# Output product by one level of Strassen's scheme: seven half-size products for eight

## The chip, the core and the metric

The kernel runs on one core of one Trainium2 chip. A core has a matrix engine (TensorE, "PE" in the profile, with its weight loads shown as "PEld"), three engines for elementwise work (VectorE or "DVE", ScalarE or "ACT", GpSimd or "POOL"), a queue engine that issues DMAs (SyncE or "SP"), a scratch memory (SBUF, 128 partitions) and a small accumulation memory that the matrix engine writes (PSUM, eight banks of 128 x 512 float32). Every engine works through its own queue strictly in the order in which the program was written; engines wait for one another through semaphores.

The metric is the time of one execution on the device, in microseconds (us); lower is better.

## The reference

There are two stages. The first is a cross attention between `x` (8 batches, 8 heads, 512 tokens, 64 features) and `state` (8, 8, 32, 64), in both directions:

```python
a     = softmax(x @ state^T / 8)        # over the 32 states
xread = a @ state                       # 512 rows for each batch
a2    = softmax(state @ x^T / 8)        # over the 512 tokens
sread = a2 @ x                          # 32 rows for each batch
```

The rows of both, with the heads side by side, make 8 x (512 + 32) = 4352 rows of 512 features. The second stage is a gated feed-forward net over them:

```python
gate = np.maximum(x @ w_gate, 0.0)      # 512 -> 1536
val  = x @ w_val                        # 512 -> 1536
out  = (gate * val) @ w_out             # 1536 -> 512
```

Inputs and outputs are float32; the kernel multiplies in bfloat16 and accumulates in float32. The last line is the output product, which the change rewrites.

## The kernel before, in words

**Units.** The 1536 hidden features are cut into 12 blocks of 128 (`jf`). For one batch and one `jf`, `gv` makes gate and value for all 512 tokens (two times two matmuls with 512 columns, into two PSUM banks), `relu` moves the gate to SBUF on ACT, and `mult` multiplies it with the value on DVE and writes the block `h_sb[:, jf]`. This is a unit, and there are 12 for each batch. A ninth round of 12 units (`gvs`, 256 columns) does the 256 state rows of all batches together.

**Output product.** It runs 18 units behind (`lag`), in pieces between the units. For a batch it is a product of 512 tokens by 1536 features with a matrix of 1536 by 512. A piece is four matmuls of 512 columns (`out_mms`, L338), and 12 pieces make the batch: four groups of 128 tokens (`tsub`), each accumulated over 12 `jf` in one of two PSUM banks of the pool `ps_o`, then copied on ACT (`fin_x`, L346) and stored from SP. The gate and value banks come from another pool of six.

**Order.** Nothing reorders the work at run time. The opening (batches 0 and 1, and the first four units of batch 2) is a list of words, `program`, where `ga` and `gb` are halves of `gv`, `o.0.4` is piece 4 of batch 0, `c` and `u` with `co` and `uo` make and copy the matrix `U`, the states already multiplied by the gate and value weights, `xn.3` is `x_next(3)`, and so on. From unit 28 on (batch 2, `jf` 4) a loop runs unit by unit, and `at(b, jf, ...)` hangs other work behind a unit: `att_half` (scores of the next batch, `sc_ps`, L184, which need `xT` of that batch), `u_block`, `sr` (sums for the state rows, `sr_ps`, L238, which for batches 0 to 2 reads `xs`), `x_sort` (GpSimd copies `xb` of batches 0 to 2 into the single buffer `xs`, L226), `x_dma` (SP loads `xf`), and `x_next`, which converts `xf` to bfloat16 on GpSimd (L149) and then transposes it by a DMA issued from SP (L156), giving `xT`.

**End.** After the last unit come the state rows' product (24 matmuls of 512 columns), the last pieces of batch 7, and `out_last`, two chains of 12 matmuls with 256 columns (L364), so that the last store is a half-width one.

Of the kernel before, what the change touches and what calls it, by code (L numbers as in the profile page):

```python
# [16 lines left out]
def kernel(  # L17
# [282 lines left out]
    def gv(b, jf, kcs=(0, 1)):  # L300
        if jf == 0 and kcs[0] == 0:
            hsb[b] = hpool.tile([128, NF, S], BF16, name="h_sb", tag="h_sb")
        if kcs[0] == 0:
            held["gv", b, jf] = [bank("gv_ps"), bank("gv_ps")], hsb[b][:, jf], S
        for w in range(2):
            for kc in kcs:
                gv_mm(held["gv", b, jf][0], b, jf, w, kc)

    def gvs(jf):
        f0 = jf * 128  # L310
        ps = [bank("gv_ps"), bank("gv_ps")]
# [5 lines left out]
        held["gv", B, jf] = ps, hs_sb[:, jf], nt  # L317

# [8 lines left out]

    o_n = [0]

    def o_bank():  # L330
        o_n[0] += 1
        return bank("o_ps", o_n[0] % 2)

    def out_mms(src, b, tsub, jfs):
        if jfs[0] == 0:
            held["o", b, tsub] = o_bank()
        for jf in jfs:
            nc.tensor.matmul(held["o", b, tsub], src[:, jf, tsub * 128:(tsub + 1) * 128], wo_sb[:, jf],  # L338
                             start=(jf == 0), stop=(jf == NF - 1))

    def out_rows(b, tsub):
        return out[b * SP: b * SP + S].rearrange("(p q) m -> q p m", q=NC)[tsub]

    def fin_x(b, tsub):
        o_sb = opool.tile([128, d_model], FP32, name="o_sb", tag="o_sb")
        nc.scalar.copy(out=o_sb, in_=held["o", b, tsub])  # L346
        nc.sync.dma_start(out=out_rows(b, tsub), in_=o_sb)

    def fin_s(t2):
        outr = out.rearrange("(b s) m -> b s m", s=SP)  # L350
        o_sb = opool.tile([128, d_model], FP32, name="o_sb", tag="o_sb")
        nc.scalar.copy(out=o_sb, in_=held["o", B, t2])
        for bq in range(4):
            eng = nc.sync if bq % 2 == 0 else nc.scalar
            eng.dma_start(out=outr[t2 * 4 + bq, S:SP], in_=o_sb[bq * Ns:(bq + 1) * Ns])

    def out_last(b, tsub):

        n = d_model // 2
        for half, (eng, q) in enumerate(((nc.scalar.copy, nc.scalar), (nc.vector.tensor_copy, nc.sync))):  # L360
            cols = slice(n * half, n * half + n)
            ps = o_bank()[:, 0:n]
            for jf in range(NF):
                nc.tensor.matmul(ps, hsb[b][:, jf, tsub * 128:(tsub + 1) * 128], wo_sb[:, jf, cols],  # L364
                                 start=(jf == 0), stop=(jf == NF - 1))
            o_sb = opool.tile([128, d_model], FP32, name="o_sb", tag="o_sb")
            eng(out=o_sb[:, 0:n], in_=ps)
            q.dma_start(out=out_rows(b, tsub)[:, cols], in_=o_sb[:, 0:n])

    def out_part(b, i):  # L370
        tsub, q = divmod(i, 3)
        out_mms(hsb[b], b, tsub, list(range(4 * q, 4 * q + 4)))

    def out_piece(b, i):
        out_part(b, i)
        if i % 3 == 2:
            fin_x(b, i // 3)

# [3 lines left out]
    nc.vector.memset(stT, 0.0)  # L382
    state_dma(nc.sync, 0, 2)
    x_dma_cast(0, 2)
# [11 lines left out]
    x_dma_cast(2)  # L396
    state_dma(nc.gpsimd, 2, B)
    wo_dma(0, 6)
# [7 lines left out]

    warm_ps = bank("warm_ps", 0)

    def spin(n):
        for i in range(n):  # L410
# [6 lines left out]
             "c": c_unit, "co": c_out, "u": u_unit, "uo": u_out, "ga": lambda b, jf: gv(b, jf, (0,)),  # L417
             "gb": lambda b, jf: gv(b, jf, (1,)), "re": relu, "mu": mult, "o": out_part,
             "of": lambda b, t, eng: fin_x(b, t), "xn": x_next}
    program = """  # L420
# [3 lines left out]
    gb.0.0 co.0.1.0.act co.1.1.1.dve ga.0.2 co.1.1.0.act gb.0.2 re.0.0 re.0.2 ga.0.3 gb.0.3 mu.0.0 ga.0.1 mu.0.2  # L424
    re.0.3 gb.0.1 re.0.1 xT.1.0 xT.1.1 xo.1.0.act mu.0.3 xT.1.2 xo.1.2.act xT.1.3 mu.0.1 xo.1.1.dve stc.2.8.pool
    xo.1.3.dve c.0.2 co.0.2.0.act sc.1.0 co.0.2.1.dve c.1.2 co.1.2.0.dve sc.1.1 ex.1.0 co.1.2.1.act ga.0.5 gb.0.5
# [22 lines left out]
    def at(b, jf, f, *args):  # L449
        units.setdefault(NF * b + jf, []).append(lambda: f(*args))  # L450
# [90 lines left out]
```

## Time and profile before

| | |
|---|---|
| time, median of 3 runs | 232.9 us (232.83 to 234.4) |
| profiled execution, span from first to last instruction | 232.8 us |
| PE busy | 224.0 us (96%) |
| DVE busy | 143.0 us (61%) |
| ACT busy | 118.8 us (51%) |
| POOL busy | 33.7 us (14%), 43 instructions |

The profiled execution has a span of 232.8 us, and the fastest of the three runs took 232.83 us, so nothing of note lies outside the span. The profile gives for each group of instructions its line, engine, operation, output and inputs by the program's names, shape, count, busy time and mean duration in ns. Matmuls overlap in the records: the duration of one (379 ns with 512 columns) is longer than the distance from one to the next, which is read from the starts of a row of them. In a timeline, the first column is the start and the second the length of a run of instructions of one kind, in us from the span's start.

### The profile page before, as it was taken

The numbers are of one execution on the slowest core, as the hardware profiler recorded it, in microseconds if no ns is written. First come the engines' busy times: TensorE is split into PE (matmuls) and PEld (weight loads), VectorE is DVE, ScalarE is ACT, GpSimd is POOL, SyncE is SP. The second block draws the span as 40 slices with busy tenths as digits, with TensorE's granted clock in tenths as the row PEclk, the third lists the DMA queues.
The fourth block names the chain that finished last, engine by engine and source line by source line (L and its number), as shares of the span: only waits on it lengthen the run. The fifth ranks groups of instructions, "written<-read, shape, count | busy, mean of one in ns | idle before, by whom it ended". The sixth has DMA issues, their size and how long they took to land.

```text
span 232.8 us, 4731 instructions
## 1 busy us (share of the span) xinstructions
PE 224.0 (96%) x1908; PEld 109.7 (47%) x1908; DVE 143.0 (61%) x246; ACT 118.8 (51%) x224; POOL 33.7 (14%) x43
## 2 busy tenths in 40 slices
PE   6699999999999999999999999999999999999994
PEld 2335445434455454345543544354445544666543
DVE  3667988974689766766676768576767463222100
ACT  2368876655655535573555355544654344332221
POOL 7936210600032312003000300000000000000000
PEclk9659999999999999999999999999999999999999
DMA  7999999033713481392139313611311111111232
GB/s 101 167 194 196 219 211 266 11 84 97 227 46 93 81 265 63 80 250 80 48 92 223 138 48 90 135 48 45 90 48 45 49 45 45 49 46 45 82 101 90
DMA packets 36951, 25.21 MB, mean 108 GB/s; under 512 B 17249, under 2 KB 32353, under 8 KB 36929
## 3 DMA queue, kind: packets, MB, share of 16 engines
q1 hardware_dynamic: 25168, 16.78, 25.4%
q0 software_dynamic: 11424, 7.73, 21.1%
q10 hardware_dynamic: 336, 0.39, 0.7%
q8 instruction: 15, 0.25, 0.4%
q14 instruction: 8, 0.06, 0.1%
HBM read 18.35 MB, written 8.91 MB: 117 GB/s over the span
## 4 chain that ended last, share of the span: by engine, by line
PE 86%; DVE 5%; DMA 4%; POOL 2%; issue 1%; ACT 1%; DVEq 0%; POOLq 0%
PE gv_ps L297 36%; PE o_ps L338 35%; PE gv_ps L315 5%; PE up L272 4%; DMA wv_sb<-in_moe_w_val_dram 3%; DVE h_sb L326 2%; PE sr_ps L238 1%; PE sr_ps L243 1%; PE sc_ps L184 1%; DVE a_sn L200 1%; PE upc L272 1%; DMA out_dram<-o_sb 1%; PE xT_ps L167 1%; POOL wg_sb L118 1%; DVE cs L194 1%
## 5 line engine op out<-in xcount | busy, mean ns | idle before, releaser
L297 PE MATMUL gv_ps<-ans,U 128*128 128x512 bf16 x384 | 97.6, 385 | 0.8 <-DVE U L292 0.5
L338 PE MATMUL o_ps<-wo_sb,h_sb 128*128 128x512 bf16 x372 | 94.7, 379 | 0.0
L322 ACT ACTIVATE g_sb<-gv_ps 128x512 bf16<-128x512 f32 (+1 forms) x108 | 62.3, 578 | 55.9 <-PE gv_ps L297 44.8
L326 DVE TENSOR_TENSOR h_sb<-gv_ps,g_sb 128x512 bf16<-128x512 f32 x96 | 64.8, 687 | 34.3 <-ACT g_sb L322 30.4
L297 PEld LDWEIGHTS <-U 128*128 128x128 bf16 x384 | 34.9, 99 | 44.8 <-issue 9.1
L338 PEld LDWEIGHTS <-h_sb 128*128 128x128 bf16 x372 | 36.1, 98 | 41.3 <-issue 0.9
L346 ACT COPY o_sb<-o_ps 128x512 f32<-128x512 f32 x31 | 18.1, 585 | 22.3 <-PE o_ps L338 22.3
L282 DVE CAST U<-up 128x512 bf16<-128x512 f32 x35 | 22.5, 684 | 6.1 <-PE up L272 6.1
L282 ACT CAST U<-up 128x512 bf16<-128x512 f32 x37 | 19.9, 594 | 9.2 <-PE up L272 9.1
L149 POOL CAST xb<-xf 128x1024 bf16<-128x1024 f32 x10 | 10.1, 1040 | 58.6 <-DMA xf<-in_x_dram 58.6
L194 DVE TENSOR_REDUCE cs<-e_sn 128x16 f32<-128x512 bf16 x16 | 10.9, 681 | 8.6 <-ACT e_sn L188 8.6
L326 DVE TENSOR_TENSOR hs_sb<-gv_ps,g_sb 128x256 bf16<-128x256 f32 x12 | 5.1, 424 | 15.4 <-PE gv_ps L315 10.5
L188 ACT ACTIVATE e_sn<-sc_ps 128x512 bf16<-128x512 f32 x16 | 9.6, 600 | 7.5 <-PE sc_ps L184 7.5
L200 DVE TENSOR_TENSOR a_sn<-e_sn,rc 128x512 bf16<-128x512 bf16 x16 | 12.5, 780 | 0.5
L272 PEld LDWEIGHTS <-stT 64*32 64x32 bf16 x480 | 4.9, 91 | 11.1 <-issue 10.5
L250 DVE RECIPROCAL rr<-sr_ps 128x128 f32<-128x128 f32 x8 | 7.6, 955 | 3.9 <-PE sr_ps L243 3.9
L226 POOL COPY xs<-xb 128x2048 bf16<-128x2048 bf16 x3 | 5.8, 1942 | 25.8 <-PE sr_ps L238 25.8
L292 ACT CAST U<-upc 128x512 bf16<-128x512 f32 x14 | 7.6, 588 | 3.7 <-PE upc L272 3.7
L184 PEld LDWEIGHTS <-xT 128*128 128x128 bf16 x128 | 6.0, 101 | 4.2 <-DVE xT L173 0.8
L184 PE MATMUL sc_ps<-stT,xT 128*128 128x64 bf16 x128 | 6.9, 199 | 0.5 <-DVE xT L173 0.5
L272 PE MATMUL up<-wg_sb,stT 64*32 64x512 bf16 x144 | 7.4, 386 | 0.0
L315 PE MATMUL gv_ps<-br,wg_sb 128*128 128x256 bf16 x48 | 7.2, 273 | 0.0
(56 smaller groups left out, 132.2 us busy)
## 6 DMA issues: line engine op xcount, KB each, us to landing
out_dram<-o_sb SPq DMA_DIRECT2D x31, 256.0 KB, 2.4
xf<-in_x_dram SPq DMA_DIRECT2D x4, 1024.0 KB, 6.4
wg_sb<-in_moe_w_gate_dram POOLq DMA_DIRECT2D x6, 256.0 KB, 11.4
wv_sb<-in_moe_w_val_dram POOLq DMA_DIRECT2D x6, 256.0 KB, 10.9
wo_sb<-in_moe_w_out_dram POOLq DMA_DIRECT2D x2, 768.0 KB, 15.1
xb<-in_x_dram POOLq DMA_DIRECT2D x2, 512.0 KB, 11.1
xf<-in_x_dram POOLq DMA_DIRECT2D x1, 1024.0 KB, 18.2
xb<-in_x_dram POOLq DMA_DIRECT2D x2, 256.0 KB, 4.6
```

Of the source, the lines that this page charges most:

```text
L149: copy[eng](out=xb[b][:, :, hs].rearrange("p c h d -> p h c d"), in_=xf[b][:, hs])
L184: nc.tensor.matmul(ps[:, c, jj], xT[b][:, c, 2 * kc + jj], stT[:, b, 2 * kc + jj], start=True, stop=True)
L194: nc.vector.reduce_sum(out=cs, in_=e_v, axis=AX.X)
L200: nc.vector.tensor_tensor(out=a_sn[b][:, kc].rearrange("p c (h n) -> p (c h) n", n=Ns), in0=e_v, in1=held["rc", b, kc].to_broadcast([128, ...
L272: nc.tensor.matmul(dst[kc][q:q + 32], stT[r:r + 64, b, j, 32 * sl:32 * sl + 32], wsb[r:r + 64, j, lo:lo + n], start=True, stop=True)
L282: copy[eng](out=U[b][:, w, kc, lo:lo + 512], in_=held["u", b, w, lo][kc])
L297: nc.tensor.matmul(ps[w], U[b][:, w, kc, f0:f0 + 128], ANS[b][:, kc].rearrange("p c t -> p (c t)"), start=(kc == 0), stop=(kc == NK - 1))
L315: nc.tensor.matmul(ps[w][:, 0:nt], wsb[:, j, f0:f0 + 128], br[:, j].rearrange("p b n -> p (b n)"), start=(j == 0), stop=(j == NJ - 1))
L322: nc.scalar.activation(out=g_sb[:, 0:n], in_=ps[0][:, 0:n], func=AF.Relu)
L326: nc.vector.tensor_tensor(out=dst, in0=ps[1][:, 0:n], in1=held["g", b, jf][:, 0:n], op=ALU.mult)
L338: nc.tensor.matmul(held["o", b, tsub], src[:, jf, tsub * 128:(tsub + 1) * 128], wo_sb[:, jf], start=(jf == 0), stop=(jf == NF - 1))
L346: nc.scalar.copy(out=o_sb, in_=held["o", b, tsub])
```

## The change

The output product of a batch is cut into two halves in each direction: 512 tokens into A1/A2 (256 each), 1536 features into two sixes of blocks, 512 outputs into two times 256. Eight products of a quarter size each would make it; Strassen's scheme in Winograd's form makes it with seven products and fifteen sums.

- **Weight sums** (`w_sum`), four in all, once: `t1`, `t2w` on DVE and `t4` and the block `b12` (in place) on GpSimd, each 128 x 1536.
- **Operand sums** (`h_sums`, `h_last`), four for each batch, on GpSimd: `s1`, `s2`, a third one written over the block `a21`, and a fourth over `a12`. Each is cut in three instructions of 128 x 512: twelve for each batch. `h_sums` is issued after `jf` 7, 9 and 11 of its own batch, `h_last` after the second half product of the next round's slot list (step `n` = 3).
- **Products.** A product is two halves of 128 token columns; a half (`o_half`) is six matmuls of 256 columns. A batch has 14 halves, `n` = 0 to 13, spread over twelve slots (`SLOTS`), still 18 units behind. They accumulate in two banks, `w` and `z`, which go on across products.
- **Output sums.** Four ACT copies of `w` for each batch (as many as before) and three DVE additions of `z` (`o_add`, 128 x 512, new). A store takes 2 x 256 columns for 128 partitions, 256 KB as before.
- **State rows.** The same scheme with 42 matmuls of 256 columns, operand sums on DVE, interleaved at the end with the last seven halves of batch 7; the last store is a full one (256 KB).
- **Room.** `xin` has one buffer and no longer two; `st_f` holds two batches, the other six are cast by their DMA, which takes `stc.2.8.pool` away; `hs_sb` goes into the `h_sb` pool. `x_next` and the next `x_dma` move from `jf` 9 and 10 to `jf` 2 and 3 for batches from 5 on.

```diff
-    xin = pool("xin", 2)
+    xin = pool("xin", 1)
+    spool = pool("spool", 2)
...
+    def w_sum(n, eng):
+        out_, in0, in1 = ((t1, b12, b11), (t2w, b22, t1), (t4, b21, t2w), (b12, b22, b12))[n]
+        {"dve": nc.vector, "pool": nc.gpsimd}[eng].tensor_tensor(out=out_, in0=in0, in1=in1, op=ALU.subtract)
+
+    PRODUCTS = ("p1", "p2", "p6", "p5", "p7", "p4", "p3")
...
+    def h_sums(b, k, eng="pool", n=2):
...
+        tt(out=s_block(b, 1, i), in0=a21, in1=a22, op=ALU.add)
+        tt(out=s_block(b, 2, i), in0=s_block(b, 1, i), in1=a11, op=ALU.subtract)
+        tt(out=a21, in0=a11, in1=a21, op=ALU.subtract)
+
+    def h_last(b, eng="pool", n=2):
+        for k in range(HF // n):
+            i = slice(n * k, n * k + n)
+            a12 = h_block(b, 1, 0, i)
+            {"dve": nc.vector, "pool": nc.gpsimd}[eng].tensor_tensor(out=a12, in0=a12, in1=s_block(b, 2, i),
+                                                                    op=ALU.subtract)
...
+    def o_half(b, n):
+        p, c = PRODUCTS[n // 2], n % 2
+        a, w = {"p1": (h_block(b, 0, 0), b11), "p2": (h_block(b, 1, 0), b21), "p3": (h_block(b, 1, 0), b22),
+                "p4": (h_block(b, 1, 1), t4), "p7": (h_block(b, 0, 1), b12),
+                "p5": (held.get(("s", b, 1)), t1), "p6": (held.get(("s", b, 2)), t2w)}[p]
+        ps = acc(b, "w" if p in ("p1", "p6", "p7", "p4") else "z")
+        for i in range(HF):
+            nc.tensor.matmul(ps[:, HM * c:HM * c + HM], a[:, i, 128 * c:128 * c + 128], w[:, i],
+                             start=(c == 0 and i == 0 and p in ("p1", "p2", "p5")), stop=(i == HF - 1),
+                             skip_group_check=True)
...
+    def o_end(b, n):
+        if n == 1:
+            o_copy(b, "r1")
+        elif n == 3:
+            o_add(b, "r1")
+            o_store(b, "r1", 0, 0)
+            h_last(b)
+        elif n == 5:
+            o_copy(b, "r2")
+        elif n == 9:
+            o_copy(b, "r3")
+            o_add(b, "r3")
+            o_store(b, "r3", 1, 1)
+        elif n == 11:
+            o_copy(b, "r4")
+            o_store(b, "r4", 1, 0)
+        elif n == 13:
+            o_add(b, "r2")
+            o_store(b, "r2", 0, 1)
+
+    SLOTS = ((0,), (1,), (2,), (3, 4), (5,), (6,), (7, 8), (9,), (), (10, 11), (12,), (13,))
...
-    re.1.7 mu.1.5 re.1.4 o.0.0 c.0.5 ...
+    re.1.7 mu.1.5 re.1.4 hs.0.0 hs.0.1 o.0.0 c.0.5 ...
-    mu.0.11 ... re.1.11 o.0.1
-    mu.1.10 o.0.2 ex.2.1 mu.1.11 c.1.4 u.2.0.0 u.2.1.0 co.1.4.1.act o.0.3 nx.2.0 co.1.4.0.dve ...
+    mu.0.11 ... re.1.11 o.0.1 hs.0.2
+    ws.0.dve mu.1.10 o.0.2 ex.2.1 mu.1.11 ws.1.dve c.1.4 u.2.0.0 u.2.1.0 co.1.4.1.act o.0.3 nx.2.0 co.1.4.0.dve ...
-    of.0.0.act xn.3 aT.2.1 o.0.4 mu.1.8 re.1.9 mu.1.9 ao.2.1.act ga.2.0 ...
+    xn.3 ws.2.pool ws.3.pool aT.2.1 o.0.4 mu.1.8 re.1.9 mu.1.9 ao.2.1.act hs.1.0 hs.1.2 hs.1.1 ga.2.0 ...
...
-            at(s, 9, x_next, b + 1)
+            at(s, 9 if b == 3 else 2, x_next, b + 1)
-            at(s, 10, x_dma, b + 2, (nc.sync,))
+            at(s, 10 if b == 3 else 3, x_dma, b + 2, (nc.sync,))
...
-        if g >= lag:
-            out_piece(*divmod(g - lag, NF))
+        if b < B and jf in (7, 9, 11):
+            h_sums(b, (jf - 7) // 2)
+        out_slot(g - lag)
...
+    h_sums(B, 0, "dve", HF)
+    rest = [n for s in SLOTS[(NF * (B + 1) - 1 - lag) % NF + 1:] for n in s]
+    for p in ("p1", 0, 0, "p2", 0, "p6", "p5", 0, 0, "p7", "p4", 0, "p3", 0):
+        s_step(p) if p else o_step(B - 1, rest.pop(0))
```

More of the change, by code (lines that the diff above doesn't have):

```diff
@@ L326, in mult @@
         nc.vector.tensor_tensor(out=dst, in0=ps[1][:, 0:n], in1=held["g", b, jf][:, 0:n], op=ALU.mult)
[L328 to L339, printed above, removed]
@@ L357, in out_last @@
[L357 to L368, printed above, removed]
@@ L370, in out_part @@
[L370 to L377, printed above, removed]
+    wo_v = wo_sb.rearrange("p (k i) m -> p k i m", k=2)
+    b11, b12, b21, b22 = (wo_v[:, k, :, HM * m:HM * m + HM] for k in range(2) for m in range(2))
+    def w_sum(n, eng):
+        out_, in0, in1 = ((t1, b12, b11), (t2w, b22, t1), (t4, b21, t2w), (b12, b22, b12))[n]
+        {"dve": nc.vector, "pool": nc.gpsimd}[eng].tensor_tensor(out=out_, in0=in0, in1=in1, op=ALU.subtract)
@@ new lines, in o_step, with out_slot, s_end @@
+    def o_step(b, n):
+        o_half(b, n)
+        o_end(b, n)
+    SLOTS = ((0,), (1,), (2,), (3, 4), (5,), (6,), (7, 8), (9,), (), (10, 11), (12,), (13,))
+    def out_slot(u):
+        b, s = divmod(u, NF)
+        for n in SLOTS[s]:
+            o_step(b, n)
+    def s_end(p):
+        outr = out.rearrange("(b s) m -> b s m", s=SP)
+        r, t, m = {"p1": ("r1", 0, None), "p2": ("r1", 0, 0), "p6": ("r2", 0, None), "p7": ("r3", 1, None),
+                   "c22": ("r3", 1, 1), "p4": ("r4", 1, 0), "p3": ("r2", 0, 1)}[p]
+        if p in ("p1", "p6", "p7", "p4"):
+            held["sr", r] = opool.tile([128, 512], FP32, name="o_sb", tag="o_sb")
+            nc.scalar.copy(out=held["sr", r][:, 0:HM], in_=held["acc", B, "w"][:, 0:HM])
+        else:
+            nc.vector.tensor_tensor(out=held["sr", r][:, 0:HM], in0=held["acc", B, "z"][:, 0:HM],
+                                    in1=held["sr", r][:, 0:HM], op=ALU.add)
+        if m is not None:
+            for bq in range(4):
+                eng = nc.sync if bq % 2 == 0 else nc.scalar
+                eng.dma_start(out=outr[t * 4 + bq, S:SP, HM * m:HM * m + HM],
+                              in_=held["sr", r][bq * Ns:(bq + 1) * Ns, 0:HM])
@@ L380, with s_step @@
+    def s_step(p):
+        o_half(B, 2 * PRODUCTS.index(p))
+        if p != "p5":
+            s_end(p)
+        if p == "p2":
+            h_last(B, "dve", HF)
+        if p == "p7":
+            s_end("c22")
     ctx.enter_context(tc.manual_schedule())
@@ L382 @@
     nc.vector.memset(stT, 0.0)
-    state_dma(nc.sync, 0, 2)
+    state_dma(nc.sync, st_f, 0, 2)
     x_dma_cast(0, 2)
@@ L396 @@
     x_dma_cast(2)
-    state_dma(nc.gpsimd, 2, B)
+    state_dma(nc.gpsimd, st_b, 2, B)
     wo_dma(0, 6)
```

87 lines of the change are left out of this document (52 added, 35 removed).

## The prediction

> **What bounds the kernel now.** The page comes first: the busy line of each engine and the chain that ended last.
>
> ```profile
> span 232.8 us, 4731 instructions
> PE 224.0 (96%) x1908; PEld 109.7 (47%) x1908; DVE 143.0 (61%) x246; ACT 118.8 (51%) x224; POOL 33.7 (14%) x43
> PE 86%; DVE 5%; DMA 4%; POOL 2%; issue 1%; ACT 1%; DVEq 0%; POOLq 0%
> ```
>
> PE is the bound, and it holds 86% of the chain. POOL looks idle. But a share over the span hides where POOL is needed, so the stages come next (columns: length, then busy us and instructions of PE, PEld, DVE, ACT and POOL, then granted clock, DMA share, GB/s).
>
> ```profile
> 4.00:8.00 4.00, 2.27 (x38) 1.42 (x36) 1.45 (x6) 0.58 (x1) 4.00 (x7) 0.92 1.34 177
> 8.00:12.00 4.00, 2.76 (x48) 1.59 (x53) 3.17 (x8) 1.82 (x4) 3.54 (x5) 0.50 1.27 167
> 12.00:16.00 4.00, 3.82 (x56) 1.39 (x41) 2.73 (x5) 2.75 (x6) 1.48 (x2) 0.50 1.43 194
> 16.00:20.00 4.00, 4.00 (x31) 1.80 (x31) 2.08 (x3) 2.25 (x5) 1.62 (x2) 0.80 1.46 196
> 36.00:48.00 12.00, 11.51 (x152) 5.47 (x151) 11.09 (x18) 8.08 (x15) 3.86 (x3) 1.00 0.40 116
> 84.00:96.00 12.00, 12.00 (x84) 5.42 (x82) 9.19 (x17) 6.73 (x13) 2.02 (x2) 1.00 0.43 136
> ```
>
> From 84 us on PE has no gap, so matmul time taken out there comes out of the span. The other rows are kept for a rival.
>
> **What the matmuls give.** The end of the timeline shows both sizes without other work between.
>
> ```profile
> 218.90 3.40 PE L338 MATMUL o_ps<-wo_sb,hs_sb 128*128 128x512 bf16 x15
> 224.08 2.75 PE L338 MATMUL o_ps<-wo_sb,h_sb 128*128 128x512 bf16 x12
> 226.67 2.78 PE L364 MATMUL o_ps<-wo_sb,h_sb 128*128 128x256 bf16 x24
> 229.55 0.42 DVE L367 COPY o_sb<-o_ps 128x256 f32<-128x256 f32 x1 [10.81 <-DMA out_dram<-o_sb]
> L364 PE MATMUL o_ps<-wo_sb,h_sb 128*128 128x256 bf16 x24 | 2.8, 273 | 0.0
> ```
>
> The state rows' 24 matmuls of 512 columns take from 218.90 to 224.08: 0.216 us each. The 24 of 256 columns have 2.78 us less one duration of 0.273 for 23 steps: 0.109 each, half of the other. A half-size product does cost half, though each matmul loads its own weights.
>
> Before: 8 batches x 48 + 24 = 408 of 512 columns, 88.0 us. After: 8 x 84 + 42 = 714 of 256, 77.8 us. **-10.2 us** if nothing stalls. A piece of 0.863 becomes a half of 0.654, with 14 for 12.
>
> **What GpSimd gets.** Twelve two-input sums of 128 x 512 for each batch, and two weight sums of 128 x 1536. The trace has no two-input instruction on POOL. The nearest rows:
>
> ```profile
> L149 POOL CAST xb<-xf 128x1024 bf16<-128x1024 f32 x10 | 10.1, 1040 | 58.6 <-DMA xf<-in_x_dram 58.6
> L127 POOL CAST st_b<-st_f 128x768 bf16<-128x768 f32 x1 | 0.8, 822 | 6.7 <-DMA st_f<-in_state_dram 6.7
> L226 POOL COPY xs<-xb 128x2048 bf16<-128x2048 bf16 x3 | 5.8, 1942 | 25.8 <-PE sr_ps L238 25.8
> ```
>
> Two casts give (1040 - 822)/256 = 0.85 ns an element on 0.17 us. One input of 512 is 0.60 us: the low end, if a second stream is free. The high end is the longest POOL row, 1.94 us. I take two passes, 2 x 0.60 = **1.2 us**, as a sum reads twice what a cast reads, and likewise 2 x 1.48 = 2.95 us for 1536. Call the first p.
>
> [...]
>
> In steady state it fits. A batch has 12 x 1.2 + 2 x 1.0 = 16.4 us of POOL, while the period was 24.1 and becomes 22.9. In the opening it doesn't, because POOL's queue there also holds the weight sums, two batches' operand sums, the three sorts and two conversions, in written order. The rows of before that matter:
>
> ```profile
> 41.80 0.69 DVE L326 TENSOR_TENSOR h_sb<-gv_ps,g_sb 128x512 bf16<-128x512 f32 x1 [0.17 <-ACT g_sb L322]
> 44.41 1.89 POOL L226 COPY xs<-xb 128x2048 bf16<-128x2048 bf16 x1
> 45.97 1.04 PE L338 MATMUL o_ps<-wo_sb,h_sb 128*128 128x512 bf16 x4
> 47.50 1.04 PE L297 MATMUL gv_ps<-ans,U 128*128 128x512 bf16 x4 [0.49 <-DVE U L292]
> 65.30 0.63 PE L238 MATMUL sr_ps<-e_sn,xs 128*128 128x64 bf16 x16
> 73.33 0.64 PE L238 MATMUL sr_ps<-e_sn,xs 128*128 128x64 bf16 x16
> 74.09 1.89 POOL L226 COPY xs<-xb 128x2048 bf16<-128x2048 bf16 x1 [5.98 <-PE sr_ps L238]
> 75.93 2.02 POOL L149 CAST xb<-xf 128x1024 bf16<-128x1024 f32 x2
> 86.89 0.40 PE L184 MATMUL sc_ps<-stT,xT 128*128 128x64 bf16 x8
> 100.03 0.95 SPq L100 DMA_DIRECT2D xf<-in_x_dram  x1
> 124.20 1.08 SPq L100 DMA_DIRECT2D xf<-in_x_dram  x1
> xT<-xb SPq DMA_TRANSPOSE x5, 4.4
> ```
>
> Before, the first sort ran at 44.41, long before its reader `sr_ps` at 65.30. Now it is queued behind batch 1's nine sums. Step by step:
>
> - `h_last(0)` needs half 3 on PE, 45.97 less three savings of 0.21 plus 0.65, and its end: 46.2, and the sums `hs.0.2`, from 42.5 on: 46.1. Start 46.5.
> - Three sums 3.6, `x_conv(3)` 2.0, `ws.2` and `ws.3` 5.9: **58.0**, when the new `b12` is there for half 8.
> - Nine sums of batch 1, 10.8, and the first sort, 1.9: **70.7**. `sr_ps` starts at 70.8 in place of 65.30. PE itself would be there at about 66: 65.30, plus 1.3 for the DVE work below, less 0.6 saved by 11 halves for 9 pieces.
> - The second `sr_ps` follows 8.03 later, as before (4 halves for 3 pieces, equal): 78.8. The single buffer `xs` frees 0.76 after that, as the rows at 73.33 and 74.09 show: 79.6. Third sort 1.9, six sums 7.2 (`hs.2.1`, `h_last(1)`), `x_conv(4)` 2.0: 90.7; the transposing DMA lands 4.4 later: **95.1**. Before, the scores of batch 4 ran at 86.89. PE would come at 78.8 + 13.56 - 0.6 = 91.8.
>
> So PE is 8.2 us late there. In general this point is 66.3 + 24 p: 24 sums' worth lie on the path, and POOL decides from p of about 0.9 on.
>
> After that POOL catches up and PE bounds again. From 86.89 on before had 145.9 us. It loses 8.2 of the 10.2 (74 pieces and the state rows, 69.0, become 93 halves, 60.8).
>
> **DVE.** Three output sums for each batch at the 0.69 of `h_sb` make 2.1 us. DVE was 9.19 of 12 in the last stage row, 77%, and goes to 86%; still beside PE. `ws.0`, `ws.1` are 1536 elements in bf16. Bounds from DVE's rows, scaled by three:
>
> ```profile
> L200 DVE TENSOR_TENSOR a_sn<-e_sn,rc 128x512 bf16<-128x512 bf16 x16 | 12.5, 780 | 0.5
> L220 DVE COPY ans<-aT_ps 128x512 bf16<-128x512 bf16 x4 | 1.7, 414 | 0.0
> 44.70 2.13 DVE L200 TENSOR_TENSOR a_sn<-e_sn,rc 128x512 bf16<-128x512 bf16 x1
> 48.95 0.69 DVE L200 TENSOR_TENSOR a_sn<-e_sn,rc 128x512 bf16<-128x512 bf16 x1
> ```
>
> At most 2.1 us, at least 1.0 with the start cost taken once; I take 1.0, all operands being bf16 as in L220. With the first output sum that is 2.7 us ahead of the copy on which `gv_ps` waited at 47.50, less the 1.44 by which `a_sn` at 44.70 was stretched, +1.3. While POOL is later anyway this costs nothing; without that cover 2.1 us, as the 0.84 already saved there goes too.
>
> The stretched row matters: `a_sn` reads two SBUF operands, runs 0.69 at 48.95, and took 2.13 while the sort ran. There are two for each batch, and three fall into 48 to 91 us (batch 2's second, batch 3's two), now against a POOL queue that is full. The wait can fall on either engine, 0 to 2.1 us on POOL's path; I take **+1.0**.
>
> **The end.** The last addition is 0.69 in place of 0.42. The last store is 256 KB and not 128 KB:
>
> ```profile
> out_dram<-o_sb SPq DMA_DIRECT2D x31, 256.0 KB, 2.4
> out_dram<-o_sb SPq DMA_DIRECT2D x1, 128.0 KB, 1.8
> xf<-in_x_dram SPq DMA_DIRECT2D x4, 1024.0 KB, 6.4
> L367 ACT COPY o_sb<-o_ps 128x256 f32<-128x256 f32 x1 | 0.4, 372 | 0.7 <-PE o_ps L364 0.7
> ```
>
> That is +0.3 and +0.6. State product p4 accumulates on the bank that ACT has just to copy after p7, which PE can't cover: 0.37 and the hand-over, 0.6. Together **+1.5**. Copies on ACT are as many as before; the converting state load, the moved tiles and the moved loads I cost at nothing, since PE's own work covers them, unless `xf` comes late (6.4 us of landing against some 20).
>
> **Sum.** 95.1 + 145.9 - 8.2 + 1.5 + 1.0 = **235.3 us**, made against the span of 232.8; the median of the runs, 232.9, is the same within 0.1.
>
> **Rivals.**
> - **A, forecast: POOL's queue delays PE in the opening**, PE bounds later. T = 206.5 + 24 p, even with before at p = 1.1; 232 to 239 for 1.05 to 1.35. Chance 0.48.
> - **B, POOL's sums are cheap** (p below about 0.9). PE never waits for them: 232.8 - 10.2 + 1.5 + 2.1 = 226.2, and 225 to 229 around it. The one-input rate speaks for it; against it, two operands. Chance 0.27.
> - **C, the pauses also cost clock.** In the stage rows PE was busy 2.27 of 4 us, and then the clock stood at 0.50 for 8 us, until some 5 us of dense work had passed. A waits about 4 us before `sr_ps` and 3.3 before `sc_ps`: each would be followed by about 5 us at half speed, 2.5 us lost, so 240 us. Against it: gaps of 0.49 in all from 36 to 48 us left the clock at 1.00. Chance 0.18. [...]
> - **D, DVE becomes the bound**: two `a_sn` for each batch stretched by 1.44 as at 44.70 take DVE from 86 to 98% of a period, and PE then waits for free banks; five batches at 2.9 make up to 14 us, 240. But POOL's sums run from `jf` 7 to the next batch's `jf` 1, `a_sn` from `jf` 3 to 6. Chance 0.05.
> - **E, half-size matmuls don't cost half**: L364 says they do. Chance 0.02; at 10% more it would be +8.
>
> **How the numbers follow.** The bounds of 1% are 230.6 and 235.2, between them being about what measurement can't tell from no change. Slower: A's upper half 0.25, C 0.18, D and E 0.07, 0.50. Within 1%: A's middle, 0.20. Faster: B 0.27 and A's low end 0.03, 0.30. The range runs from B's 226 to C's 241, and A alone is 232 to 239.
>
> **What would show it.** Right: POOL busy without a break from about 46 to 91 us, PE waiting for POOL `xs` at the first `sr_ps` and for the transposed `xT` of batch 4, POOL sums of 1.1 to 1.3 us, later batches 1.2 us shorter than 24.1. Wrong: POOL sums under 0.9 us, or PE at 100% from 50 us on; then it is B. A clock under 1.00 after the waits is C; PE waiting for DVE in later batches is D.

## The result and the profile after

The changed kernel takes **242.36 us** (median of 4 runs, 241.87 to 242.79), the kernel before 233.47 us beside it: a ratio of **1.0374, 95% interval 1.0332 to 1.0416**. It is slower by 3.7%, and above the top of the forecast range. One execution of 799.4 us, of the kernel in "The loads alone", is left out of every figure below.

The page of the changed kernel: span, busy line, and the chain that ended last by engine.

```profile
span 241.0 us, 5460 instructions
PE 216.8 (90%) x2174; PEld 140.7 (58%) x2202; DVE 163.0 (68%) x278; ACT 119.9 (50%) x226; POOL 149.9 (62%) x140
PE 64%; POOL 18%; DMA 9%; DVE 4%; issue 3%; ACT 1%; ACTq 0%; DVEq 0%; POOLq 0%
```

PE does less work than before (216.8 us busy, before 224.0), and the span is 8.2 us longer. PE's share of the chain fell from 86% to 64%; POOL has 18% and the DMA 9%. So TensorE now waits. Its list of waits (engine, line, what it waited for: total us, how often, longest):

```profile
PE sr_ps L240 <- POOL xs L228: 3.4, 1, 3.4
PE gv_ps L299 <- DVE U L294: 2.8, 1, 2.8
PE gv_ps L299 <- DMA ans<-a_sn: 2.4, 1, 2.4
PE sc_ps L186 <- DMA xT<-xb: 1.6, 1, 1.6
...
PE ws_ps L388 <- ACT o_sb L446: 1.2, 1, 1.2
```

Before, TensorE waited 0.49 us for `U` and for none of the others. Each happens once, four of the five in the opening or in the round of batch 4. The rows of the timeline that set the points of the path (start, length, then what was waited for):

```profile
71.52 1.04 PE L240 MATMUL sr_ps<-e_sn,xs 128*128 128x64 bf16 x16 [3.38 <-POOL xs L228]
...
96.46 0.41 PE L186 MATMUL sc_ps<-stT,xT 128*128 128x64 bf16 x8 [1.65 <-DMA xT<-xb]
...
114.42 1.04 PE L299 MATMUL gv_ps<-ans,U 128*128 128x512 bf16 x4 [2.41 <-DMA ans<-a_sn]
115.30 1.29 PE L388 MATMUL z_ps<-t,s 128*128 128x256 bf16 x6
...
123.72 0.40 PE L186 MATMUL sc_ps<-stT,xT 128*128 128x64 bf16 x8
...
146.67 0.40 PE L186 MATMUL sc_ps<-stT,xT 128*128 128x64 bf16 x8
...
169.62 0.40 PE L186 MATMUL sc_ps<-stT,xT 128*128 128x64 bf16 x8
```

Read the first scores of each batch, `sc_ps`, as mile posts. From 146.67 to 169.62 a round takes 22.95 us: that is the new period, 1.2 under the 24.1 of before, and it holds from 123.72 on. The first state read starts at 71.52 (before 65.30), the scores of batch 4 at 96.46 (before 86.89). But the round from 96.46 to 123.72 takes 27.26, 4.3 more than the others. In it stands the wait for `ans`, 2.41, and the half product behind it (six matmuls, at 115.30) takes 1.29 where one otherwise takes 0.82. The stages show why (columns as in the prediction):

```profile
108.00:116.00 8.00, 5.53 (x60) 2.97 (x46) 4.21 (x7) 4.34 (x8) 7.84 (x8) 0.97 0.87 214
116.00:120.00 4.00, 3.95 (x44) 3.07 (x44) 1.08 (x2) 0.20 (x1) 4.00 (x4) 0.64 0.01 4
```

The granted clock, last but two, was 0.64 after the wait, though PE was busy for 3.95 of these 4 us. So of the 4.3 us, 2.4 are the wait and most of the other 1.9 the clock. One of the runs below ("The weight sums on VectorE") has nearly the same wait at this point without the fall of the clock:

```profile
114.28 1.04 PE L299 MATMUL gv_ps<-ans,U 128*128 128x512 bf16 x4 [2.68 <-DMA ans<-a_sn]
115.16 0.82 PE L388 MATMUL z_ps<-t,s 128*128 128x256 bf16 x6
```

There the granted clock stays at 1.00, and from this `gv_ps` to the next scores it takes 7.67 us, where the changed kernel takes 9.30. So 1.6 of the 4.3 are clock.

What made `ans` late stands in SyncE's queue. First the changed kernel, with the conversion on GpSimd and the `a_sn` on VectorE that the two transposing DMAs wait for; then the kernel before at the same point of its round:

```profile
100.52 2.02 POOL L151 CAST xb<-xf 128x1024 bf16<-128x1024 f32 x2 [5.08 <-DMA xf<-in_x_dram]
101.94 1.14 DVE L202 TENSOR_TENSOR a_sn<-e_sn,rc 128x512 bf16<-128x512 bf16 x1
```

```profile
102.57 1.71 SPq L158 DMA_TRANSPOSE xT<-xb  x1
104.33 1.19 SPq L404 DMA_DIRECT2D out_dram<-o_sb  x1
105.61 0.43 SPq L102 DMA_DIRECT2D xf<-in_x_dram  x1
106.14 0.82 SPq L404 DMA_DIRECT2D out_dram<-o_sb  x1
107.05 3.73 SPq L210 DMA_TRANSPOSE ans<-a_sn  x1
```

```profile
93.66 1.24 SPq L208 DMA_TRANSPOSE ans<-a_sn  x1
97.47 0.34 SPq L347 DMA_DIRECT2D out_dram<-o_sb  x1
97.91 2.07 SPq L156 DMA_TRANSPOSE xT<-xb  x1
100.03 0.95 SPq L100 DMA_DIRECT2D xf<-in_x_dram  x1
```

Before, the load of x (1 MB) followed the transposing DMA of `ans` by 6.4 us. Now the transposing DMA of `xT`, the load and two stores stand ahead of it. `a_sn` was done at 103.08, but `xT` waited in the queue for the conversion, which ended at 102.54, and `ans` was issued only at 107.05: 4.0 us lost. Its issue then takes 3.73 in place of 1.24, and it lands 7.3 us after it started, where the median of the five such DMAs of this run is 3.3. In the next round the load stands ahead of `ans` as well, but 4.3 us ahead (125.87 and 130.17), and the issue takes 1.29.

### The profile page after: what moved, and what is told of

It reads as the page before. It is cut to its first block, busy times and chain, and to the rows that moved or that the text cites. A ratio compares the mean times of both kernels' runs of the same rounds, so it can differ in the third digit from the quotient of the medians.

```text
span 241.0 us, 5460 instructions
## 1 busy us (share of the span) xinstructions
PE 216.8 (90%) x2174; PEld 140.7 (58%) x2202; DVE 163.0 (68%) x278; ACT 119.9 (50%) x226; POOL 149.9 (62%) x140
## 4 chain that ended last, share of the span: by engine, by line
PE 64%; POOL 18%; DMA 9%; DVE 4%; issue 3%; ACT 1%; ACTq 0%; DVEq 0%; POOLq 0%
PE gv_ps L299 28%; PE w_ps L388 12%; PE z_ps L388 11%; PE gv_ps L317 4%; DMA ans<-a_sn 3%; DVE h_sb L330 3%; DMA wv_sb<-in_moe_w_val_dram 3%; POOL s L361 3%; POOL h_sb L369 3%; POOL s L360 2%; POOL h_sb L362 2%; PE up L274 2%; DMA xT<-xb 2%; POOL xb L151 2%; PE sr_ps L240 2%
## 5 line engine op out<-in xcount | busy, mean ns | idle before, releaser
L330 DVE TENSOR_TENSOR h_sb<-gv_ps,g_sb 128x512 bf16<-128x512 f32 (+1 forms) x108 | 69.6, 657 | 35.7 <-ACT g_sb L326 20.4
L360 POOL TENSOR_TENSOR s<-h_sb 128x512 bf16<-128x512 bf16 x24 | 27.7, 1153 | 50.2 <-DVE h_sb L330 50.2
L369 POOL TENSOR_TENSOR h_sb<-h_sb,s 128x512 bf16<-128x512 bf16 x24 | 28.2, 1199 | 8.2 <-PE z_ps L388 8.2
L397 ACT COPY o_sb<-w_ps 128x512 f32<-128x512 f32 x32 | 18.8, 587 | 23.0 <-PE w_ps L388 19.8
L361 POOL TENSOR_TENSOR s<-s,h_sb 128x512 bf16<-128x512 bf16 x24 | 28.3, 1178 | 1.9
L362 POOL TENSOR_TENSOR h_sb<-h_sb 128x512 bf16<-128x512 bf16 x24 | 28.1, 1172 | 0.0
L388 PE MATMUL w_ps<-wo_sb,h_sb 128*128 128x256 bf16 x192 | 26.9, 277 | 0.5 <-POOL wo_sb L338 0.5
L388 PE MATMUL z_ps<-wo_sb,h_sb 128*128 128x256 bf16 x192 | 26.2, 273 | 0.2
L388 PEld LDWEIGHTS <-s 128*128 128x128 bf16 x204 | 20.1, 99 | 6.5
L401 DVE TENSOR_TENSOR o_sb<-z_ps,o_sb 128x512 f32<-128x512 f32 x24 | 16.4, 683 | 3.9 <-ACT o_sb L397 3.3
```

The source lines that it names most:

```text
L330: nc.vector.tensor_tensor(out=dst, in0=ps[1][:, 0:n], in1=held["g", b, jf][:, 0:n], op=ALU.mult)
L360: tt(out=s_block(b, 1, i), in0=a21, in1=a22, op=ALU.add)
L361: tt(out=s_block(b, 2, i), in0=s_block(b, 1, i), in1=a11, op=ALU.subtract)
L362: tt(out=a21, in0=a11, in1=a21, op=ALU.subtract)
L369: {"dve": nc.vector, "pool": nc.gpsimd}[eng].tensor_tensor(out=a12, in0=a12, in1=s_block(b, 2, i), op=ALU.subtract)
L388: nc.tensor.matmul(ps[:, HM * c:HM * c + HM], a[:, i, 128 * c:128 * c + 128], w[:, i], start=(c == 0 and i == 0 and p in ("p1", "p2", "p5" ...
```

## The experiments

Each kernel is the changed one with the edit shown, unless another is named. "Before" is the kernel before on the same chip, beside which each was timed; the ratios are to it.

**The sort first.** In the written opening the first sort stands ahead of batch 1's sums, where it needs nothing new.

```diff
-    re.1.7 mu.1.5 re.1.4 hs.0.0 hs.0.1 o.0.0 ...
+    re.1.7 mu.1.5 re.1.4 hs.0.0 hs.0.1 xs.0 o.0.0 ...
-    for b in range(3):
+    for b in range(1, 3):
         at(2, 4 + 2 * b, x_sort, b)
```

> The first sort (x_sort of batch 0) is written before batch 1's nine sums, in a stretch where POOL waits for DVE anyway (35 to 41 us). Theory POOL queue (the order of GpSimd's queue makes PE wait at the first sr_ps, 71.5 us, and through the third sort and the conversion of batch 4 at sc_ps, 96.5 us): the wait of 3.4 us at the first sr_ps goes, it starts near 68; sc_ps of batch 4 near 93; time 3 to 4.5 us less, 238 to 239.5. Rival, PE and DVE set the pace there: the first sr_ps moves but nothing after it, time within 1 us of 242.4.

Measured: 238.65 us, ratio 1.0214 (1.0174 to 1.0253), 3.7 us less than the changed kernel, as expected. From the timeline and from the list of waits:

```profile
67.88 0.63 PE L240 MATMUL sr_ps<-e_sn,xs 128*128 128x64 bf16 x16
```

```profile
PE sc_ps L186 <- DMA xT<-xb: 2.5, 1, 2.5
PE gv_ps L299 <- DMA ans<-a_sn: 2.3, 1, 2.3
```

The first state read starts without a wait, 3.6 us earlier, and the scores of batch 4 come 3.7 us earlier, at 92.72. The delay that POOL's queue makes in the opening reaches the end in full. The wait for `ans` stays as it was, so it has another cause.

**The weight sums on VectorE.** This takes 6.2 us out of POOL's queue.

```diff
-    xn.3 ws.2.pool ws.3.pool aT.2.1 ...
+    xn.3 ws.2.dve ws.3.dve aT.2.1 ...
```

> The two weight sums ws.2 and ws.3 run on DVE and not on GpSimd. Theory POOL queue: POOL's path to the first sr_ps loses 6.2 us (3.09 and 3.10), DVE gets two times 0.97; the first sr_ps waits no more, sc_ps of batch 4 is near 93, time 238 to 239.5. Rival, DVE is what holds PE in the opening: 2 us of added DVE work make it 243 to 244.5.

Measured: 241.73 us (239.42 to 244.06), ratio 1.0316 (1.0243 to 1.0388). The expected gain is not there. POOL was no longer waited for, yet the first state read came at 72.06. The timeline of VectorE and the waits show what took its place:

```profile
50.62 1.53 DVE L202 TENSOR_TENSOR a_sn<-e_sn,rc 128x512 bf16<-128x512 bf16 x1
52.07 0.41 DVE L222 COPY ans<-aT_ps 128x512 bf16<-128x512 bf16 x1
52.41 1.45 DVE L338 TENSOR_TENSOR t<-wo_sb,t2w 128x1536 bf16<-128x1536 bf16 x1
53.78 1.90 DVE L338 TENSOR_TENSOR wo_sb<-wo_sb 128x1536 bf16<-128x1536 bf16 x1
55.61 1.27 DVE L330 TENSOR_TENSOR h_sb<-gv_ps,g_sb 128x512 bf16<-128x512 f32 x2
```

```profile
PE gv_ps L299 <- DVE h_sb L330: 2.8, 3, 2.2
```

The two sums hold the `h_sb` behind them by 3.3 us, and PE waits 2.2 for it. The same work blocks VectorE and TensorE directly instead of late through POOL.

**Filling the pause.** Twelve matmuls of 512 columns that nothing reads stand before the first state read, 2.6 us. They add work; the output stays what it was.

```diff
     def sr(b):
+        if b == 0:
+            dummy = bank("dummy_ps")
+            for i in range(12):
+                nc.tensor.matmul(dummy, id128, wo_sb[:, 0], start=True, stop=True)
         sr_mm(b)
```

> Twelve matmuls of 512 columns whose result nobody reads (2.6 us of PE) are put just ahead of the first sr_ps. The output is the same. Theory POOL queue: they fall into PE's wait of 3.4 us and the time doesn't rise, 242.4 within 0.7, and is up to 1.5 lower if the pause cost clock there (granted clock 0.68 from 72 to 76 us goes to 1.00). Rival, PE is on the path there: plus 2.6, 245.

Measured: 242.82 us (242.77 to 243.25), ratio 1.0399 (1.0361 to 1.0438). Work of 2.6 us costs 0.5, and the intervals of the two ratios overlap. The timeline (this execution ran 1.5 us later from the opening on: its scores of batch 3 start at 67.77, those of the changed kernel at 66.23):

```profile
69.52 2.75 PE L559 MATMUL dummy_ps<-wo_sb,id 128*128 128x512 bf16 x12
73.07 0.64 PE L240 MATMUL sr_ps<-e_sn,xs 128*128 128x64 bf16 x16 [0.80 <-POOL xs L228]
73.54 0.63 PE L245 MATMUL sr_ps<-e_sn,sel 128*128 128x64 bf16 x16
```

The wait shrank to 0.80, and the state read's 16 matmuls took 0.64, against 1.04 after the wait of 3.38. So that wait did cost clock too, which was 0.68 from 72 to 76 us in the changed kernel: from the first state read to the second it is 9.11 us in the changed kernel, 8.31 here, 8.03 before. That is 0.8 us of clock for a wait of 3.4. It shows that PE had the slack. It doesn't show that the clock alone was worth anything for the end, as POOL was still late for what follows.

**The moved loads back.** Conversion and load of x stand where the kernel before has them.

```diff
-            at(s, 9 if b == 3 else 2, x_next, b + 1)
+            at(s, 9, x_next, b + 1)
-            at(s, 10 if b == 3 else 3, x_dma, b + 2, (nc.sync,))
+            at(s, 10, x_dma, b + 2, (nc.sync,))
```

> x_next and x_dma go back to jf 9 and 10 for all batches, as in the kernel before; one xin buffer stays. Theory, SP's order: the 1 MB load xf now stands ahead of the transposing DMA of ans in batch 4's round, which was issued at 107.05 and took 3.7 us to issue and 7.3 to land, so that gv_ps waited 2.4 us at 114 us, and the clock fell after it; with the load later the wait goes, time 4 us less, 238.5. Rival, that loss comes from DVE or POOL being late: time unchanged, 242.4, or higher because the conversion now comes late for the transposing DMA.

Measured: 242.23 us (241.83 to 243.46), ratio 1.0383 (1.0328 to 1.0439): nothing gained. The wait for `ans` is gone, but another came, in each later batch. The list of waits:

```profile
PE sc_ps L186 <- DMA xT<-xb: 4.8, 4, 1.8
```

There are four of them here; in the changed kernel it was one. The scores of batches 4 to 7 start at 96.71, 120.80, 144.91 and 168.97, 24.1 us apart. That is exactly the period of before: the conversion, now behind POOL's sums, takes back per batch what the products save. So the conversion had to be moved; what cost was the place of the moved DMAs in SyncE's queue. Here `ans` is issued at 102.94, as soon as `a_sn` is done (102.88), and lands within 3.2.

**The load behind `ans`.** Only the load, not the conversion, is put later, behind the transposing DMA.

```diff
-            at(s, 10 if b == 3 else 3, x_dma, b + 2, (nc.sync,))
+            at(s, 10 if b == 3 else 6, x_dma, b + 2, (nc.sync,))
```

> One move in SP's queue: x_dma of the batch after the next goes from jf 3 to jf 6, so that the 1 MB load stands behind the transposing DMA of ans (jf 5) and not ahead of it. Theory, the load ahead of it made ans late: the wait of 2.4 us of gv_ps at 114 us goes, and the clock stays at 1.00 after it (1.9 us): 238 to 239.5. Rival, ans is late because xT of batch 5 and the stores ahead of it wait (xf late at 100.5 us): the wait stays, 242.4.

Measured: 239.32 us (239.07 to 240.23), ratio 1.0237 (1.0196 to 1.0278), 3.0 us less in time; the span is 237.3, 3.7 less. SyncE's queue now:

```profile
104.69 1.73 SPq L404 DMA_DIRECT2D out_dram<-o_sb  x2
106.51 2.58 SPq L210 DMA_TRANSPOSE ans<-a_sn  x1
109.18 0.53 SPq L102 DMA_DIRECT2D xf<-in_x_dram  x1
```

The wait for `ans` is gone, the clock stayed at 1.00 from 108 to 132 us, and the scores of batch 5 start at 119.97, where they had been at 123.72. The other waits are the changed kernel's. `ans` still stands 3.1 us in the queue behind `xT` and two stores (`a_sn` is done at 103.45), and the slowest of the five `ans` DMAs lands after 5.4. So the load was not all of the delay, but enough of it for the wait to go. This is the part that the prediction had left out.

**The loads alone.** The kernel *before* with only the two moved lines of the change.

```diff
-            at(s, 9, x_next, b + 1)
+            at(s, 9 if b == 3 else 2, x_next, b + 1)
-            at(s, 10, x_dma, b + 2, (nc.sync,))
+            at(s, 10 if b == 3 else 3, x_dma, b + 2, (nc.sync,))
```

> The kernel before, with nothing of the change but the moved loads: the conversion of the next x (x_next) at unit 2 and the load behind it (x_dma) at unit 3 of each slice but one, as the changed kernel has them. Theory 'the load ahead in SyncE's queue costs the wait for ans by itself': TensorE waits 2 to 3 us for ans in the round of batch 4, the clock dips there, and the time goes up by 2.5 to 4.5 us, to 236 to 238. Rival 'it takes GpSimd's sums too': without them GpSimd is free, xf(4) is converted earlier, the load behind it is issued and landed before the transposing DMA of ans is, and the time stays within 1 us of 233.5.

Measured: 234.20 us (median of nine runs), ratio 0.9993 (0.9968 to 1.0018): no difference. Its queue at the same place:

```profile
89.67 1.29 SPq L100 DMA_DIRECT2D xf<-in_x_dram  x1
91.22 0.42 SPq L347 DMA_DIRECT2D out_dram<-o_sb  x1
93.45 1.24 SPq L208 DMA_TRANSPOSE ans<-a_sn  x1
```

The load stands ahead of `ans` here too, but 3.8 us ahead and not 1.4, and the issue of `ans` takes its 1.24. So the rival was right: the order alone costs nothing. The rows suggest that it needs POOL's late conversion: the load and `ans` stand in the queue behind the `xT` of that conversion, which ended at 88.26 here, 1.5 us after the scores of batch 4 began (86.72), but at 102.54 in the changed kernel, 6.1 after them (96.46). This kernel also keeps two buffers for `xf`, which was not tried apart; but in both kernels the load is issued behind that `xT`, when a buffer is free with one as with two. Which of the load and the stores beside it slowed the transposing DMA was not tried apart either.

**The end.** One output slot stands between state products p7 and p4, so that ScalarE can copy p7 meanwhile.

```diff
-    for p in (..., "p5", 0, 0, "p7", "p4", 0, "p3", 0):
+    for p in (..., "p5", 0, 0, "p7", 0, "p4", "p3", 0):
```

> In the order of the end, half 12 of batch 7 goes between state products p7 and p4, so that ACT copies the bank of p7 meanwhile. Theory: the wait of 1.2 us at ws_ps goes or shrinks, time 0.5 to 1.2 less, 241.2 to 241.9. Rival, the last store and not PE sets the end, or the o_sb buffers do: unchanged within 0.3.

Measured: 243.02 us (241.26 to 244.27), ratio 1.0383 (1.0318 to 1.0447): no gain, though the four runs spread over 3.0 us, more than the gain looked for. The traces are clearer: the wait before p4 fell from 1.2 to 0.6, and from the scores of batch 7 to the end it is 71.4 us in both (169.62 to 241.0, 171.05 to 242.5). SyncE's queue of this kernel at the end:

```profile
236.14 3.08 SPq L453 DMA_DIRECT2D out_dram<-o_sb  x6
239.31 0.39 SPq L404 DMA_DIRECT2D out_dram<-o_sb  x1
```

The six small stores of the state rows hold the queue for 3.08 us, and the last large store follows right behind them. That these stores and not TensorE set the end is what the rows suggest; no run moved the stores.

**The repairs together.** The sort first, the load behind `ans`, the order at the end (as in the edits above), and for batch 4 the load (`xd.4`) and the conversion behind it earlier.

```diff
-    re.1.7 mu.1.5 re.1.4 hs.0.0 hs.0.1 o.0.0 ...
+    re.1.7 mu.1.5 re.1.4 hs.0.0 hs.0.1 xs.0 o.0.0 ...
-    xn.3 ws.2.pool ...
+    xn.3 xd.4 ws.2.pool ...
-    at(2, 4, x_dma, 4, (nc.sync,))
...
-            at(s, 9 if b == 3 else 2, x_next, b + 1)
+            at(s, 4 if b == 3 else 2, x_next, b + 1)
-            at(s, 10 if b == 3 else 3, x_dma, b + 2, (nc.sync,))
+            at(s, 6, x_dma, b + 2, (nc.sync,))
```

> First sort early as in e1, x_dma behind ans as in e5, the end as in e6, and x_dma of batch 4 right behind x_next(3), x_next(4) at jf 4 of batch 2 (ahead of the other sorts), x_dma of batch 5 at jf 6. Theory, POOL's and SP's order cost what the losses of PE say: sc_ps of batch 4 waits no more (2.5 us in e1), the ans wait and its clock go (4.3), the end shrinks by about 1: 238.7 less 6.5 to 8, 231 to 232.5, about even with before or a little faster. Rival, the cost is POOL's amount of work and not its order: the waits turn up at other places and it stays above 235.

Measured: 234.02 us (10 runs), ratio **1.0000** (0.9976 to 1.0024). Of the waits listed for the changed kernel only VectorE's 2.8 for `U` and 0.6 before p4 are left. The scores of batch 4 start at 92.34. The loss of the change, 8.3 us, is gone, so it came from the order in two queues; without it the change is worth nothing. The expectation, 231 to 232.5, was missed, and so was its rival, above 235. What the earlier load and conversion of batch 4 give by themselves was not timed.

**The weight sums earlier as well.** The edit is made to the kernel of the repairs. `ws.0` and `ws.3` stand behind `co.1.5.0`, `ws.1` behind the copies of the third slice's first unit.

```diff
-    ... co.1.5.0.dve gb.0.10
+    ... co.1.5.0.dve ws.0.dve ws.3.pool gb.0.10
-    ws.0.dve mu.1.10 ... mu.1.11 ws.1.dve c.1.4 ... co.1.4.0.dve uo.2.0.0.1.dve
+    mu.1.10 ... mu.1.11 c.1.4 ... co.1.4.0.dve uo.2.0.0.1.dve ws.1.dve
-    xn.3 xd.4 ws.2.pool ws.3.pool aT.2.1 ...
+    xn.3 xd.4 ws.2.pool aT.2.1 ...
```

> As e7, and the weight sums moved: ws.0 earlier on DVE, ws.3 on GpSimd ahead of hs.0.2, where POOL waits for DVE, ws.1 behind the copies of U on DVE. Theory: PE's wait of 2.8 us for U at 48.8 us shrinks by 1.5 to 2.5, 229 to 231, faster than before by 1 to 2%. Rival, DVE's amount of work in 36 to 52 us holds PE whatever the order: no gain over e7.

Measured: 233.13 us (10 runs), ratio **0.9958** (0.9933 to 0.9982). This is the best version, and its gain is 0.4%; 229 to 231 was expected. PE's wait for `U` did not shrink, it grew from 2.8 to 3.05. The rows of PE and VectorE around it:

```profile
49.51 1.89 PE L299 MATMUL gv_ps<-ans,U 128*128 128x512 bf16 x4 [3.05 <-DVE U L294]
```

```profile
46.56 0.69 DVE L401 TENSOR_TENSOR o_sb<-z_ps,o_sb 128x512 f32<-128x512 f32 x1 [1.67 <-PE z_ps L388]
47.17 1.68 DVE L202 TENSOR_TENSOR a_sn<-e_sn,rc 128x512 bf16<-128x512 bf16 x1
48.77 0.68 DVE L294 CAST U<-upc 128x512 bf16<-128x512 f32 x1
49.37 0.68 DVE L284 CAST U<-up 128x512 bf16<-128x512 f32 x1
49.97 1.81 DVE L338 TENSOR_TENSOR t2w<-wo_sb,t 128x1536 bf16<-128x1536 bf16 x1
```

The new output sum (L401) waits 1.67 for PE at the head of VectorE's queue, and the copies of `U` wait behind it and behind an `a_sn` of 1.68. The obvious next step is to put the copies first.

**The copies first.** The kernel of the weight sums with this edit, and then the same with the changed kernel's own order at the end:

```diff
-    ... co.1.4.1.act o.0.3 nx.2.0 co.1.4.0.dve uo.2.0.0.1.dve ws.1.dve
+    ... co.1.4.1.act co.1.4.0.dve uo.2.0.0.1.dve o.0.3 nx.2.0 ws.1.dve
```

> This is the kernel of e8_weight_sums with VectorE's two copies of the third slice's first unit (U, L294 and L284) put ahead of its output sum (o_sb, L401) and of the scaling of a_sn (L202). In e8 the copy of L294 ended at 49.45 us because the output sum before it in VectorE's order waited 1.67 us for TensorE and the scaling took 1.68 us under GpSimd's sums; TensorE waited 3.05 us for the copy. Theory 'order on VectorE': with the copy first the wait falls under 0.6 us, the clock holds in 48 to 60 us (it was 0.86), and the time goes down by 2.5 to 4.5 us, to 228.5 to 230.5. Rival 'the waits are the only room GpSimd's sums have': the product b12 and the operands of the first state read become the next that is late, the wait moves to sr_ps and the time stays within 1 us of 233.1. Rival 'a_sn now late': aT waits instead (0.9 us before) and half of the gain is left, 231.5.

> The kernel of e9_copy_first with the changed kernel's own order at the end (p7, p4, an output slot, p3). Theory from e6_tail (the small stores on the DMA queue of SyncE and not TensorE set the end): the same time as e9 within 0.6 us. Rival (the products' order sets the end): 1 us later than e9.

Measured: 233.57 us, ratio 0.9969 (0.9943 to 0.9994), and with the changed kernel's own end 233.48 us, 0.9980 (0.9952 to 1.0008). Neither is better than the kernel of the weight sums, and the two ends are the same, as the run on the end had it. The gain of 2.5 to 4.5 us isn't there. The wait for `U` is gone, but TensorE's list now has

```profile
PE aT_ps L218 <- DVE a_sn L202: 4.2, 3, 2.2
```

The rival "`a_sn` now late" was the right kind, and worse than it priced. In 45 to 53 us, in each of the two orders tried, another of VectorE's operations is late: they only move the wait. That VectorE has too much there in any order isn't shown; an order that removes the wait was not found.

## Why the prediction was wrong

- **Price of POOL's sums, right.** I took p = 1.2 between 0.60 and 1.94. In the profile's groups (busy, mean ns) it is 1.15 to 1.20:

```profile
L360 POOL TENSOR_TENSOR s<-h_sb 128x512 bf16<-128x512 bf16 x24 | 27.7, 1153 | 50.2 <-DVE h_sb L330 50.2
L369 POOL TENSOR_TENSOR h_sb<-h_sb,s 128x512 bf16<-128x512 bf16 x24 | 28.2, 1199 | 8.2 <-PE z_ps L388 8.2
```

  The weight sums took 3.1 us each, 2.95 was said. Rival B, p below 0.9, is out by the 1.15 to 1.20 alone.
- **POOL's queue in the opening, right.** Said: first state read at 70.8, scores of batch 4 at 95.1 plus 1.0. Measured: 71.52 and 96.46. "The sort first" shows that this is the queue and not the amount: 3.7 us went by moving one copy. That the sum fits within 0.4 is luck in part. POOL's chain began at 45.74, 0.8 earlier than said, and its sums of 1.15 were shorter than 1.2; against that, three sums took 4.54 (3.37 later on), the conversion 2.48 (2.02) and the sort 2.36 (1.89), with VectorE busy for 4.47, 2.44 and 1.20 us of these, and the clock cost 0.8 between the two state reads. PE itself was later too: by its own work it would have been at the scores of batch 4 at 94.8, where I had 91.8. So the waits were 3.38 and 1.65; my own sums gave 70.8 - 66.0 = 4.8, which I called "about 4", and 3.3. And POOL was not busy without a break: between 71 and 82 us it was idle three times, 1.23, 1.25 and 1.56.
- **The matmuls, right.** The period went from 24.1 to 22.95, said 22.9. Rival E is out.
- **"The moved loads I cost at nothing", wrong, and this is the step that failed.** I had the condition, "unless `xf` comes late", and then checked only the landing of `xf` against PE's work. The moves have a second effect, on the transposing DMA of `ans` behind them in the same queue: it was held 4.0 us behind `xT`, the load and the stores, and then took 7.3 to land for 3.3. That cost 4.3 us in the round of batch 4, 2.4 as a wait and 1.6 as clock. "The load behind `ans`" takes 3.0 us out of the time. "The loads alone" has the moves without the rest of the change and no wait for `ans`; "The moved loads back" has POOL's sums without the moves and no wait for `ans` either. So it takes both, the new places and, as the rows suggest, POOL's late conversion.
- **The end, too small.** +1.5 was said. From the scores of batch 4 on, the changed kernel has 144.5 us (241.0 less 96.46); said were 145.9 - 8.2 + 1.5 = 139.2. Of the 5.3 between them 4.3 are the round above; 1.0 is left, by difference, so the end cost 2.5. I priced the hand-over before p4 at 0.6, and it took 1.2, as the copy on ACT itself waited 0.85 for a store to free its buffer; but "The end" shows that removing half of this is no gain. That the 1.0 lies in the stores is what their rows suggest, and isn't shown.
- **The base, wrong by 1.8.** I held the span of 232.8 to be the time. The profiled execution of the changed kernel took 242.79 us with a span of 241.0, and all later ones had about 1.8 outside the span as well, the kernel before too (234.34 with a span of 232.5). So what stands ahead of the prediction, that nothing of note lies outside the span, doesn't hold, and my 235.3 was a span. Median less span is 1.4 here (242.36 - 241.0). The error then adds up: 0.4 up to the scores of batch 4, 4.3 and 1.0 behind them, 1.4 outside, 7.1 in all.
- **Rival C, half right.** Its place and sign were right, its price (2.5 us for each wait, 240 us in all) too high: 0.8 after the wait of 3.4, 1.6 after that of 2.4, and nothing after the wait of 2.76 for `U` and that of 1.65 for `xT`, which left the clock at 1.00. The forecast A should have held a clock term for its own waits, and C was not an alternative to A but a part of it.
- **Rival D, wrong as told.** The later batches run without a wait for VectorE. TensorE did wait for it, but in 45 to 53 us of the opening.

Where the 10.2 us of saved products went in the best version: its scores of batch 4 start at 90.71, 3.8 later than before, though about 2.0 of the saving lies ahead of them, so 5.8 are lost there, all behind 43 us, where the two kernels are still level. Of these, 2.6 are the wait for `U` (3.05 for 0.49), and at most 1.7 the clock, which was 0.86 from 48 to 60 us (0.14 x 12); part of this fell into the wait itself. Of the other 1.5, 0.5 is a wait for `a_sn` at 53 us, and the rest I can't assign. From there to the end it has 140.3 us for 145.9, a gain of 5.6. Opening and rest nearly cancel; 1.8 us of span are left, and 1.0 between the medians (233.13 against 234.15 for the kernel before on that chip).

## What to carry to other kernels

Work that is moved to an idle engine enters that engine's queue, and its price is paid by whatever stands behind it (3.7 us here, by "The sort first"): list the readers of everything queued behind, down to the buffers that come free later and the DMAs that are then issued later. Of a moved load ask not only when it lands but which DMA follows it in the same queue, and how close (here 1.4 us ahead, with 3.73 to issue, or 3.8, with 1.24). And when several waits of 2 to 4 us are forecast, the clock that may be lost after each (here 0.8 us after 3.38, 1.6 after 2.41, nothing after 2.76), with its chance, belongs in the main sum, not in a rival.

## What the runs showed of the hardware

- The same 1536-element bf16 sum took 3.10 us on POOL and 0.95 on VectorE while POOL was idle, but 1.45 to 1.90 on VectorE while POOL ran its conversion and sums; the 512-element `a_sn` went from 0.69 to as much as 1.68. The added time, 0.5 to 1.0, is at most one POOL sum of 1.15. A POOL sum was longer beside one on VectorE too: in the changed kernel one L361, from 42.91 on, took 1.76 for 1.15, while a weight sum ran on VectorE from 42.68 in 0.97.
- A transposing DMA with a load of 1 MB issued 1.4 us ahead of it, between two stores, took 3.73 to issue and 7.3 to land; with the load 3.8 us ahead of it (in the kernel before) it took 1.24 to issue. With the load behind it, but two stores just ahead, it took 2.58, and nothing waited.
- The granted clock of a 4 us stage fell to 0.64 after a wait of 2.41 us, and the half product behind it took 1.29 for 0.82, while PE was busy for 3.95 of the 4. In steps of 1 us from 114.42 the clock was 1.00, 0.54, 0.50, 0.50, 0.76, 1.00: 1.7 us lost in all. But a wait of this size doesn't always do it. Behind the wait for `U`, 2.7 to 2.8 in each, the granted clock from 48 to 60 us was 0.86 in "The sort first", "Filling the pause" and "The repairs together", and 1.00 in the changed kernel and in "The moved loads back", "The load behind `ans`" and "The end". In "The weight sums on VectorE" it was 0.92, where the half product behind a second wait, of 2.21, took 1.44 for 0.82. What decides it, these runs don't show.
